# Half of the strided tensors loaded as whole 72 rows, the other half as 64 rows and a shared rest

## Chip, cores, metric

Trainium2, one core. The metric is the device time of one execution in microseconds (us).

## The reference, cut to what matters

```python
def reference(q, k, v, moe_w_r, moe_w_i, moe_w_ch):        # shortened by the author
    # q, k, v: [8 batches, 8 heads, 576, 64] float32; w_r, w_i: [64 modes, 512, 512]; w_ch: [512, 512]
    # heads 0..3: local mask (the last 32 positions); heads 4..7: strided mask (same position mod 32)
    attn = softmax(where(mask, q @ k^T / 8, -1e9)) @ v
    x = attn as [8, 576, 512]
    X = rfft(x, axis=1);  Y = zeros_like(X)
    Y[:, m] = X[:, m] @ (w_r[m] + 1j * w_i[m])             # 64 modes, each with its own weights
    u = x + irfft(Y)
    return u + relu(u @ w_ch)
```

The 64 modes' weights are most of what is loaded; the strided heads' inputs are loaded first.

Of the kernel before, what the change touches and what calls it, by code (L numbers as in the profile page):

```python
# [77 lines left out]
def kernel(  # L78
# [71 lines left out]
    ring = pat.tile([128, 12, 2048], F16, name="ring")  # L150
# [43 lines left out]



    SRC = {2: v, 0: q, 1: k}
    SLOT = {2: 0, 0: 1, 1: 2}

    def str_in(b, vi):  # L200
        return ring[0:72, 3 * (b % 4) + SLOT[vi], :]

    def loc_in(b, vi):
        t = ring[:, ds(2 * (b % 6), 2), :].rearrange("p n x -> p (n x)")
        return t[:, ds(1152 * vi, 1152)]

    def load_str(b):
        for vi in (2, 0, 1):
            nc.gpsimd.dma_start(
                str_in(b, vi)[0:64],  # L210
                SRC[vi][b, 4:8].rearrange("h (c r) d -> (h c) (r d)", r=32)[0:64],
            )
            if b % 2 == 0:
                n = 3 * (b % 4) + SLOT[vi]
                nc.gpsimd.dma_start(
                    ring[64:72, n : n + 4 : 3, :],
                    SRC[vi][b : b + 2, 4:8].rearrange(
                        "b h (c r) d -> (h c) b (r d)", r=32
                    )[64:72],
                )  # L220

    def load_loc(*bs):
        for b in bs:
            if b >= B:
                return
            for vi in (2, 0, 1):
                nc.gpsimd.dma_start(
                    loc_in(b, vi),
                    SRC[vi][b, 0:4].rearrange("h (cb i) d -> (h cb) (i d)", i=18),
                )  # L230
# [465 lines left out]

    psum_pools(tp=3, sc=3, av=2)
    load_str(0)
    const_load(nc.scalar, "cI", "cM6", "cM5", "cFs")
    load_str(1)  # L700
    const_load(nc.sync, "cMl", "cFl", "cA")
    load_str(2)
    w_fetch(2)

# [63 lines left out]
    for b in range(B):  # L768
# [12 lines left out]
        n = 0  # L781
        nm = NMODES[b]
        for mi in range(nm):
# [3 lines left out]
            n = upto  # L787
# [43 lines left out]
    n = 0  # L831
# [3 lines left out]
    for m in range(NM - 3):  # L835
# [7 lines left out]
        n = upto  # L843
# [99 lines left out]
    for i in range(len(units)):  # L943
        v_rows(i)
        b, t = units[i]
# [42 lines left out]
```

## The kernel before, where the change touches it

For a strided head, 576 positions are 18 rows of 32 positions. Four heads of one batch make 4 x 18 = 72 rows; one row is 32 x 64 numbers, read as float32 (8 KB) and written to SBUF as float16 (4 KB), one row to a partition. Each row is one packet in the trace (17,984 of 4,096 bytes on GpSimd's queue in the kernel before, as many as it has strided rows and weight rows). The kernel before loads the first 64 rows of each tensor alone, and the last 8 rows of two successive batches together ("the rest").

```python
    SRC = {2: v, 0: q, 1: k}
    SLOT = {2: 0, 0: 1, 1: 2}

    def str_in(b, vi):
        return ring[0:72, 3 * (b % 4) + SLOT[vi], :]
    # ... cut: loc_in
    def load_str(b):
        for vi in (2, 0, 1):
            nc.gpsimd.dma_start(
                str_in(b, vi)[0:64],
                SRC[vi][b, 4:8].rearrange("h (c r) d -> (h c) (r d)", r=32)[0:64],
            )
            if b % 2 == 0:
                n = 3 * (b % 4) + SLOT[vi]
                nc.gpsimd.dma_start(
                    ring[64:72, n : n + 4 : 3, :],
                    SRC[vi][b : b + 2, 4:8].rearrange(
                        "b h (c r) d -> (h c) b (r d)", r=32
                    )[64:72],
                )
```

The weights come on the same queue of GpSimd, each also as 64 rows of 4 KB:

```python
    def w_fetch(n=1):
        for _ in range(n):
            # ... cut: which buffer
            for ri, src in enumerate([moe_w_r, moe_w_i] if m else [moe_w_r]):
                nc.gpsimd.dma_start(
                    wt[ds(64 * ri, 64)],
                    src[m, ds(256 * half, 256), :].rearrange("(p c) e -> p c e", c=4),
                )
# ... cut
    load_str(0)
    load_str(1)
    load_str(2)          # constants between these are cut
    w_fetch(2)
# ... cut
    for b in range(B):   # the strided stage
        if b < 5:
            load_str(b + 3)
        load_loc(*[(), (), (), (), (0,), (1, 2), (3,), (4, 5)][b])
        w_fetch([3, 3, 2, 2, 2, 1, 1, 1][b])
        # ... cut: the attention of batch b
```

The softmax here doesn't subtract the row's maximum and nothing guards it: scores larger than these inputs give would overflow.

## Time and profile before

| kernel before | |
|---|---|
| time, first 3 runs | 439.35 us (439.08 to 439.46) |
| span of the profiled run | 437.8 us |
| moved by DMA, counted as written | 92.35 MB, mean 211 GB/s |
| GpSimd's DMA queue | 26,800 packets, 94.1% of 16 engines' time |
| 21st weight load complete | 63.24 us |
| last weight load complete | 396.36 us |

A load counts as complete when the last of its 16 completions has come. These are rows of the table of stretches of the kernel before; the last three columns are the granted TensorE clock, the mean busy share of the DMA engines (a row is recorded as 322 to 324 ns long and the next one starts 304 ns after it, so it can pass 1) and the GB/s moved.

```profile
11.00:22.00 11.00, 10.48 (x146) 9.07 (x145) 8.96 (x20) 7.04 (x14) 5.88 (x12) 1.00 1.06 210
22.00:33.00 11.00, 8.70 (x156) 7.11 (x157) 9.41 (x26) 9.07 (x20) 4.73 (x9) 1.00 1.06 212
33.00:44.00 11.00, 8.44 (x126) 7.25 (x126) 8.29 (x24) 7.07 (x16) 6.00 (x12) 0.84 1.06 210
```

A share of 1.06 with 210 to 212 GB/s is what full engines with undisturbed rows look like here.

### The profile page before, as it was taken

How to read it: one execution, taken by the hardware profiler on the slowest of the kernel's cores; microseconds unless marked ns; L12 is line 12 of the kernel's file. 1: busy time of each engine (PE TensorE's matmuls, PEld its weight loads, DVE VectorE, ACT ScalarE, POOL GpSimd, SP SyncE). 2: the span in 40 equal slices, each digit the busy share in tenths (PEclk: the TensorE clock that was granted, in tenths of full speed). 3: DMA queues.
4: the chain of work that ended last, by engine and by line, in shares of the span. 5: the costliest groups of instructions: out<-in, count | busy, mean ns of one | idle time of the engine just before them, and what ended most of it. 6: DMA issues, size and time to landing. Idle time of an engine off the chain costs nothing.

```text
span 437.8 us, 12314 instructions
## 1 busy us (share of the span) xinstructions
PE 338.0 (77%) x5284; PEld 240.9 (55%) x5284; DVE 215.6 (49%) x463; ACT 188.6 (43%) x353; POOL 186.8 (43%) x339
## 2 busy tenths in 40 slices
PE   1977787689895888989765475778586958997994
PEld 1866676567784666766644344445454635654441
DVE  2887788844543333353311134354335434753895
ACT  1686688625543445444432211134022402443882
POOL 6545453333344344444343444343444444310883
PEclk9998999967986657686875559696777868988998
DMA  8999999999999999999999999999999999990687
GB/s 186 211 211 212 211 213 209 211 210 211 213 211 212 213 208 211 213 212 211 211 212 211 213 212 210 213 213 210 201 211 212 211 212 213 211 192 15 264 324 277
DMA packets 31094, 92.35 MB, mean 211 GB/s; under 512 B 6144, under 2 KB 7040, under 8 KB 31040
## 3 DMA queue, kind: packets, MB, share of 16 engines
q0 software_dynamic: 26800, 81.29, 94.1%
q1 hardware_dynamic: 3440, 9.50, 5.8%
q10 hardware_dynamic: 800, 0.77, 0.6%
q8 instruction: 42, 0.69, 0.6%
q14 instruction: 12, 0.10, 0.1%
HBM read 163.37 MB, written 9.44 MB: 395 GB/s over the span
## 4 chain that ended last, share of the span: by engine, by line
DMA 74%; PE 15%; DVE 4%; issue 4%; POOL 1%; ACT 0%; DVEq 0%; POOLq 0%
DMA wt<-in_moe_w_i_dram 54%; DMA wt<-in_moe_w_r_dram 12%; DMA ring<-in_v_dram 4%; DMA ring<-in_q_dram 4%; PE sc L634 3%; PE v L884 2%; PE v L669 2%; PE u L684 2%; PE y L536 1%; DVE yy L663 1%; PE u L903 1%; PE tp L313 1%; POOL wt L183 1%; PE tp L642 1%; DVE xT L586 1%
## 5 line engine op out<-in xcount | busy, mean ns | idle before, releaser
L536 PE MATMUL y<-X,wt 128*128 128x16 f16 (+1 forms) x2048 | 82.2, 192 | 59.0 <-DMA wt<-in_moe_w_i_dram 57.1
L183 POOL DMA_DIRECT2D wt<-in_moe_w_r_dram x128 | 65.8, 514 | 118.8 <-DMA wt<-in_moe_w_r_dram 35.6
L536 PEld LDWEIGHTS <-wt 128*128 128x128 f16 (+1 forms) x2048 | 72.0, 103 | 72.7 <-issue 51.7
L183 POOL DMA_DIRECT2D wt<-in_moe_w_i_dram x126 | 64.8, 514 | 67.5 <-DMA wt<-in_moe_w_i_dram 50.0
L643 ACT ACTIVATE v<-sc 128x512 f16<-128x512 f32 x32 | 18.9, 597 | 88.4 <-PE sc L634 88.4
L634 PE MATMUL sc<-w_cp,xT 128*128 128x512 f16 (+1 forms) x160 | 52.5, 459 | 0.5 <-DVE xT L606 0.4
L460 ACT ACTIVATE PL<-sc 128x480 f16<-128x480 f32 (+1 forms) x48 | 27.5, 579 | 48.1 <-PE sc L446 47.8
L644 DVE COPY xo<-tp 128x512 f16<-128x512 f16 x32 | 22.1, 692 | 42.4 <-PE tp L642 42.4
L239 DVE TENSOR_TENSOR xb<-av,rec 90x256 f16<-90x256 f32 (+2 forms) x80 | 36.0, 450 | 2.7
L238 DVE RECIPROCAL rec<-av 90x4 f32<-90x4 f32 (+2 forms) x80 | 14.7, 184 | 40.1 <-PE av L475 29.3
L391 DVE COPY qT<-tp 128x576 f16<-128x576 f16 x16 | 12.0, 758 | 39.9 <-PE tp L384 37.0
L249 ACT ACTIVATE v<-tp 128x640 f16<-128x640 f16 (+1 forms) x24 | 19.4, 807 | 21.5 <-PE tp L418 18.1
L349 ACT ACTIVATE PL<-sc 90x360 f16<-90x360 f32 (+1 forms) x48 | 22.8, 490 | 9.8 <-PE sc L342 9.1
L897 POOL TENSOR_TENSOR rl<-rl,xo 128x512 f32<-128x512 f32 x16 | 18.4, 1159 | 20.2 <-ACT rl L895 19.4
L384 PE MATMUL tp<-cI_s,ring 64*64 64x64 f16 x864 | 26.1, 211 | 1.0 <-DVE qT L391 0.6
L914 DVE TENSOR_TENSOR osb<-u,rl 128x512 f32<-128x512 f32 x36 | 23.9, 689 | 3.1 <-ACT zz L662 1.9
L430 PE MATMUL sc<-cMl_s,cI_s 128*128 128x480 f16 (+1 forms) x48 | 23.1, 481 | 1.6 <-ACT X L249 1.6
L384 PEld LDWEIGHTS <-ring 64*64 64x64 f16 x864 | 20.7, 123 | 6.2 <-issue 3.4
L446 PE MATMUL sc<-qT,kz 128*128 128x160 f16 (+1 forms) x160 | 23.4, 275 | 0.8 <-issue 0.8
L634 PEld LDWEIGHTS <-xT 128*128 128x128 f16 (+1 forms) x160 | 14.8, 110 | 14.9 <-issue 7.2
L446 PEld LDWEIGHTS <-kz 128*128 128x128 f16 x160 | 16.7, 118 | 11.3 <-issue 8.8
L274 PE MATMUL tp<-cI_s,ring 72*128 72x72 f16 x256 | 15.1, 207 | 10.1 <-DMA ring<-in_v_dram 7.7
(98 smaller groups left out, 647.1 us busy)
## 6 DMA issues: line engine op xcount, KB each, us to landing
wt<-in_moe_w_r_dram POOLq DMA_DIRECT2D x128, 256.0 KB, 9.4
wt<-in_moe_w_i_dram POOLq DMA_DIRECT2D x126, 256.0 KB, 9.6
out_dram<-osb SPq DMA_DIRECT2D x14, 512.0 KB, 2.7
ring<-in_v_dram POOLq DMA_DIRECT2D x8, 288.0 KB, 10.3
ring<-in_q_dram POOLq DMA_DIRECT2D x8, 288.0 KB, 10.7
ring<-in_k_dram POOLq DMA_DIRECT2D x8, 288.0 KB, 10.3
ring<-in_v_dram POOLq DMA_DIRECT2D x8, 256.0 KB, 8.0
ring<-in_q_dram POOLq DMA_DIRECT2D x8, 256.0 KB, 8.3
```

The source lines that it names most:

```text
L183: nc.gpsimd.dma_start(wt[ds(64 * ri, 64)], src[m, ds(256 * half, 256), :].rearrange("(p c) e -> p c e", c=4),)
L239: nc.vector.tensor_tensor(out=dst, in0=val.rearrange("p h (q c) -> p h c q", c=4), in1=rec[0:n, 0:pieces] .to_broadcast((n, pieces, 64)) . ...
L249: nc.scalar.activation(out=out, in_=in_, func=ACTF.Copy)
L349: nc.scalar.activation(out=PS[0:n, ds(POFF[t], 4 * n)], in_=scp[0:n, 0 : 4 * n], func=ACTF.Exp, scale=SCALE,)
L384: nc.tensor.transpose(tp[ds(64 * hp, 64), ds(64 * i, 64)], qn[ds(64 * hp, 64), ds(64 * (9 * g + i), 64)], idn[ds(64 * hp, 64), ds(64 * hp, ...
L430: nc.tensor.matmul(scp[:, 0 : n * times].rearrange("p (h x) -> p h x", h=times), idn, mask_rows("cMl", n, times), start=True, stop=False,)
L446: nc.tensor.matmul(scp[:, ds(col, n)], kzs[par][:, hp, ds(s0, 128)], qTs[par][:, ds(s0, n)], start=False, stop=(i == len(todo) - 1),)
L460: nc.scalar.activation(out=dst, in_=src, func=ACTF.Exp, scale=SCALE)
L536: nc.tensor.matmul(yv[:, mi, e, :], wt[pr, XC[c], ds(128 * e, 128)], Xh[half][pr, c, :, :, m], start=(c == 0), stop=(c == 3),)
L634: nc.tensor.matmul(vp[pr, :], xT[:, ch, cols], w_chs["cp"][:, ch, :], start=(ch == 0), stop=(ch == 3),)
L644: nc.vector.tensor_copy(out=xo[pr].rearrange("p (h q c) -> p h q c", h=2, c=4), in_=tp[pr, 0:512].rearrange("p (h c q) -> p h q c", h=2, c=4),
L914: nc.vector.tensor_tensor(out=osb[:, t % 2, :], in0=up, in1=rls[b, t][:, t % 2, :], op=AluOp.add)
```

## The change

The intent is fewer DMA issues and fewer small transfers: half of the (batch pair, tensor) combinations load all 72 rows in one transfer, and only the other half keeps 64 rows and the shared rest.

```diff
     def load_str(b):
         for vi in (2, 0, 1):
+            n = 64 if (b // 2 + SLOT[vi]) % 2 == 0 else 72
             nc.gpsimd.dma_start(
-                str_in(b, vi)[0:64],
-                SRC[vi][b, 4:8].rearrange("h (c r) d -> (h c) (r d)", r=32)[0:64],
-            )
-            if b % 2 == 0:
-                n = 3 * (b % 4) + SLOT[vi]
+                str_in(b, vi)[0:n],
+                SRC[vi][b, 4:8].rearrange("h (c r) d -> (h c) (r d)", r=32)[0:n],
+            )
+            if n == 64 and b % 2 == 0:
+                i = 3 * (b % 4) + SLOT[vi]
                 nc.gpsimd.dma_start(
-                    ring[64:72, n : n + 4 : 3, :],
+                    ring[64:72, i : i + 4 : 3, :],
                     SRC[vi][b : b + 2, 4:8].rearrange(
                         "b h (c r) d -> (h c) b (r d)", r=32
                     )[64:72],
```

## The prediction

> **What bounds the kernel now.** I read the sliced part of the page first, for the engines and the DMA.
>
> ```profile
> PE   1977787689895888989765475778586958997994
> ...
> DMA  8999999999999999999999999999999999990687
> GB/s 186 211 211 212 211 213 209 211 210 211 213 211 212 213 208 211 213 212 211 211 212 211 213 212 210 213 213 210 201 211 212 211 212 213 211 192 15 264 324 277
> ...
> q0 software_dynamic: 26800, 81.29, 94.1%
> ```
>
> No compute engine is full for long, but the DMA engines are full from the second slice to the 35th (about 11 to 383 us), at 208 to 213 GB/s with one dip to 201. The software queue, which GpSimd feeds, carries 94% of it. The strided loads that change sit in the first 61 us of this stream; the weights follow on the same queue. Next the chain of work that ended last, from its late part:
>
> ```profile
> 326.86 0.28 issue
> 327.14 9.64 DMA wt<-in_moe_w_i_dram
> ...
> 356.60 0.28 issue
> 356.88 9.64 DMA wt<-in_moe_w_i_dram
> 366.65 0.65 PE y L536 x16
> 367.30 0.86 PE sc L634 x4
> ```
>
> Columns are start, length and what (us). Until 366.5 us the chain is one weight load after another; each is issued when the one eight places before it has landed (the Pool's DMAs use eight semaphores in turn), so one link of 9.64 us spans eight loads of 1.24 us that stream without a hole. From 366.65 us it is TensorE and VectorE work. The timeline of TensorE shows the change-over:
>
> ```profile
> 359.25 0.64 PE L536 MATMUL y<-X,wt 128*128 128x16 f16 x16 [1.28 <-DMA wt<-in_moe_w_i_dram]
> ...
> 366.65 0.65 PE L536 MATMUL y<-X,wt 128*128 128x16 f16 x16 [0.80 <-DMA wt<-in_moe_w_i_dram]
> ...
> 372.46 0.65 PE L536 MATMUL y<-X,wt 128*128 128x16 f16 x16
> ...
> 397.22 0.64 PE L536 MATMUL y<-X,wt 128*128 128x16 f16 x16
> ```
>
> The bracket is idle time and what ended it. Mode 51 (at 366.65) is the last that waits for its weights; its load landed at 366.52. What follows is a fixed tail of 437.8 - 366.6 = 71.2 us. So the kernel ends a fixed time after one landing, and whatever delays the DMA stream by x before then delays the end by x.
>
> **A closer reading of the landings.** Every load posts 16 completions, one from each DMA engine, and the trace's completion records show when. In the steady stage, first and last completion of one load lie 4.1 to 4.6 us apart: the 16 engines run at their own pace, and the slowest sets each landing. The packet records tell why. A 4 KB row follows the one before it on its engine after 304 ns, and a completion takes 21 ns: 4 x 304 + 21 = 1237 ns for a load of 64 rows over 16 engines, which is the 1.24 us step between landings. Following packets in chains, every engine gets 4 rows of every 64-row load. Of the 8-row rest (two batches, 16 rows) eight engines get 2 rows each and the other eight none, and the two halves take turns from rest to rest. Twelve rests make six turns each, so before is even: by the sizes, 17,984 rows over 16 engines are 1,124 each. What spreads the engines is 42 instruction fetches of 16 KB (about 0.95 us each), whose durations repeat with period eight: they fall on eight engines. Near 55 us the first and the last completion both belong to the half that is served second, and the fetch gaps that I could follow are on that half too. These eight late engines end within about 1.2 us of each other, at 395 to 396 us, the other eight at 392. The slowest never runs dry: where GpSimd was held up for 3.4 us near 152 us, the early engines lost their lead but the last landings kept their 1.24 us step.
>
> [...]
>
> **The change part by part.** Bytes are the same. The DMA issues:
>
> ```profile
> ring<-in_v_dram POOLq DMA_DIRECT2D x8, 256.0 KB, 8.0
> ring<-in_q_dram POOLq DMA_DIRECT2D x8, 256.0 KB, 8.3
> ring<-in_k_dram POOLq DMA_DIRECT2D x8, 256.0 KB, 8.3
> ...
> ring<-in_v_dram POOLq DMA_DIRECT2D x4, 64.0 KB, 7.7
> ring<-in_q_dram POOLq DMA_DIRECT2D x4, 64.0 KB, 7.3
> ring<-in_k_dram POOLq DMA_DIRECT2D x4, 64.0 KB, 6.9
> ```
>
> These are 24 loads of 64 rows and 12 rests. After: 12 loads of 64, 12 of 72, 6 rests.
> 1. Removed: six issues. On GpSimd that is 6 x 0.57 us = 3.4 us, but GpSimd waits for landings anyway, so nothing of it is on the path. On each DMA engine a rest costs up to two small packets, 2 x 21 ns: 6 x 42 = 0.25 us gained, on the path.
> 2. Moved: which engine carries the rows. [...]
> 3. If instead fourteen engines take 5 rows: 12 x 4 + 12 x 5 + 3 x 2 = 114 rows, 6 more than 108: 6 x 0.304 = 1.82, less 0.25: **+1.6 us**.
> 4. Earlier inputs: two batches' slots no longer have to be free before a rest is issued, for half of the rests, and half the tensors land in one piece. TensorE waits once for strided data for long (7.7 us at the start), but this stage ends far ahead of its weights; the first wait for weights comes later, so nothing on the path.
>
> **The rivals.** *The rows are spread evenly after all*[...]: then only part 1 remains, 439.1 us. For it: the change looks meant as a saving of issues; against it: 72 isn't a multiple of 16, and somebody chose 64 plus a rest. *Twelve engines*: 442.6 us[...]. *Sixteen engines with 5 rows*: 441.0[...]. *GpSimd is the limit at the start*, so that fewer issues start the stream earlier: in the timeline the first eight issues follow each other in 0.5 to 0.7 us each, and each 64-row load holds the engines for 1.24 us; the queue is never short, and I give it 0.3 us at most. *A longer lag empties the queue*: with 3.6 us more, the spread of 4 to 5.8 us would near the 9.9 us that eight loads hold; the early engines then stop more often, the late ones don't, so no further cost.
>
> **Range and chances.** Weights 0.35 for twelve engines (+3.3), 0.45 for sixteen with 5 rows (+1.6), 0.2 for an even spread (-0.2) give 0.35 x 3.3 + 0.45 x 1.6 - 0.2 x 0.2 = +1.8; I stay near the most likely case and put 441.0 us. The range from 438.9 to 443.0 holds all three with the scatter between runs, which was 0.4 us. A change of 2% is 8.8 us, over twice the largest of these: faster by over 2% has 0.01, slower by over 2% has 0.02, within has 0.97.
>
> **What would show it right or wrong.** The slices of DMA should stay at 208 to 213 GB/s, the chain should still run over weight loads until near 367 us plus the loss, and mode 51's neighbours should still be the last to wait. The last weight landing, now 396.4 us, should move by as much as the end. In the completion records the spread between first and last should be wider after the strided stage (after 61 us): by up to 3.6 us with twelve engines, by 2 with sixteen, with one engine that races ahead. In the packet records rows in a load of 72 should come as runs of 6 on twelve engines, or of 5. Wrong would be: an unchanged spread and the time at 439.1 (even spread); a time above 443.5 (the late engine runs dry, or the compute in the strided stage came onto the path); or a gain of over 1 us, which would mean that the row was taken off the engines that are late.

The kernel before has no load of 72 rows, so its trace doesn't say how they spread: the three cases and their weights are estimates. The forecast's sum: 0.35 x 3.3 (twelve engines) + 0.45 x 1.6 (part 3) - 0.2 x 0.2 (part 1 alone) = +1.8 us. It was put at part 3's +1.6, which is 441.0 us.

Two of its readings have more figures in the trace of the kernel before. Turns: two steps alternate. At its rests from the second on, the load's first completion came 0.33, 0.17, 0.50, 0.17, 0.50, 0.18, 0.62, 0.18, 0.59, 0.21 and 0.57 us after that of the transfer before. Instruction fetches: most durations follow 893, 948, 945, 935, 974, 974, 961, 893 ns and again from the start; that they fall on eight engines is read from this period. 42 x 0.95 / 8 = 5.0 us on each of these, beside a spread of 4.1 to 4.6 us, so that they are what spreads the engines is an estimate.

## More of the kernel before

The experiments ran on three chips (e1 to e4 on one, e5 to e11 on another, e12 and e13 on a third), each beside the kernel before on the same chip; each loss is taken against that chip's own runs of it. Of the kernel before there is one profile, so counts from profiles are compared across chips.

All strided inputs but the three of the last batch (in by 70.1 us) are in before the 21st weight load, so its time is the state of the stream near the end of the stage that the change touches.

## The result and the profile after

| | before | after |
|---|---|---|
| median of 6 runs | 439.40 us (438.39 to 439.86) | 443.42 us (442.33 to 445.02) |
| span of the profiled run | 437.8 us | 441.5 us |
| 21st weight load complete | 63.24 us | 68.00 us (+4.8) |
| last weight load complete | 396.36 us | 401.57 us (+5.2) |

The ratio is 1.010, 95% interval 1.0075 to 1.0125: slower by 1%, inside the 2% that counts as the same. A ratio here and below is the mean time of one kernel's fast runs over the mean of the other's of the same rounds, so it is not quite the ratio of the medians quoted. The +4.0 us lie above the predicted +1.6 and 0.4 us above the range.

First the page of the changed kernel, the sliced lines and the queue:

```profile
DMA  8999999999999999999999999999999999991687
GB/s 179 181 197 200 210 196 202 211 211 212 211 211 211 214 210 205 209 215 211 213 209 212 212 213 211 212 213 212 210 190 211 212 212 211 212 212 37 264 316 279
...
q0 software_dynamic: 26704, 81.29, 94.6%
```

The busy digits of the early slices are unchanged: 9 from the second on. But the GB/s of the first seven slices read 179 to 202 with one 210, where before they were 209 to 213 from the second on. Engines as busy as before move less. From the eighth slice on both kernels look alike. The queue has 96 packets fewer and yet takes 94.6% of a longer span.

The stretches of the changed kernel say it more sharply (columns as above):

```profile
11.00:22.00 11.00, 9.34 (x112) 8.39 (x110) 7.11 (x15) 4.78 (x9) 4.78 (x9) 1.00 1.12 180
22.00:33.00 11.00, 9.41 (x172) 7.71 (x170) 9.21 (x25) 9.04 (x19) 3.80 (x8) 1.00 1.09 196
33.00:44.00 11.00, 8.58 (x155) 6.77 (x151) 9.41 (x26) 8.31 (x19) 4.92 (x10) 1.00 1.07 202
```

In the first row the DMA share went up from 1.06 to 1.12 while the rate fell from 210 to 180. Busy time per byte is share over rate: (1.12 / 180) / (1.06 / 210) = 1.23, so a byte cost 23% more engine time. In the next two rows it is 11% and 5%. If engines had only been short of work, or some had more rows than others, the share would have fallen with the rate. So packets took longer.

The packet records give the same thing row by row. A 4 KB row of GpSimd's queue is recorded as lasting 322 to 324 ns in both kernels (its neighbours start 304 ns apart). Of those in the first 80 us, 32 of 3,456 lasted over 344 ns before, and 689 of 3,357 after, 368 of them over 400 ns. I call these slow rows; of the 689, 574 lasted from 345 to 500 ns.

The completion records also show how 72 rows are spread. These are, for four loads of the changed kernel in their order, the 16 completions in us after the load's first:

```
before, 8th   0.0 0.4 0.8 0.9 0.9 1.1 1.1 1.1 1.1 1.2 1.2 1.3 1.5 1.5 1.8 1.8
after,  7th   0.0 0.4 2.6 2.6 2.7 2.8 2.9 3.0 3.0 3.2 3.2 3.3 3.3 3.7 3.7 3.9
after,  9th   0.0 1.4 4.6 4.7 4.7 4.8 4.9 5.0 5.1 5.2 5.3 5.4 5.4 5.7 5.8 5.9
after, 12th   0.0 1.6 5.8 5.9 5.9 6.1 6.1 6.2 6.2 6.2 6.3 6.4 6.6 6.6 7.2 7.3
```

Two engines race ahead, one more than the other, and fourteen stay together; twelve engines with 6 rows would have left four ahead. At the 12th, after four loads of 72, the two lead the third by 5.8 and 4.2 us, or 1.45 and 1.05 us a load: at 304 ns a row that is about 5 and 3 to 4 rows. So I read the 72 rows as 5 on fourteen engines, 2 on one and none on one.

The issues, from the view of the DMA:

```profile
ring<-in_q_dram POOLq DMA_DIRECT2D x12, 288.0 KB, 10.5
ring<-in_v_dram POOLq DMA_DIRECT2D x12, 288.0 KB, 10.4
ring<-in_k_dram POOLq DMA_DIRECT2D x12, 288.0 KB, 10.7
...
ring<-in_v_dram POOLq DMA_DIRECT2D x2, 64.0 KB, 7.4
```

The x12 are the 8 local inputs of each tensor and four whole 72-row loads, which happen to have the same size; of the rests two are left per tensor. All as intended.

The late chain keeps its form, one link per eight weight loads, and the change-over to TensorE comes 5.3 us later (366.65 before). From the chain and from TensorE's timeline of the changed kernel:

```profile
352.32 9.62 DMA wt<-in_moe_w_i_dram
362.22 9.64 DMA wt<-in_moe_w_i_dram
```

```profile
371.99 0.65 PE L538 MATMUL y<-X,wt 128*128 128x16 f16 x16 [0.43 <-DMA wt<-in_moe_w_i_dram]
374.87 0.66 PE L538 MATMUL y<-X,wt 128*128 128x16 f16 x16
```

The chain's shares differ more than its end does. The line of the page before and the line after:

```profile
DMA 74%; PE 15%; DVE 4%; issue 4%; POOL 1%; ACT 0%; DVEq 0%; POOLq 0%
```

```profile
DMA 63%; PE 23%; DVE 6%; issue 4%; ACT 1%; POOL 1%; DVEq 0%; POOLq 0%; ACTq 0%
```

The extra compute in the chain stands between 73 and 122 us: there a load was issued when TensorE freed a buffer, not when an earlier load landed. It is no loss by itself: slices 8 to 12 are at 211 to 212 GB/s, so the engines still had work. Of the +5.2 us at the last weight load, 4.8 were there at 68 us.

### The profile page after: what moved, and what is told of

It reads as the page before. It is cut to its first block, busy times and chain, and to the rows that moved or that the text cites. A ratio compares the mean times of both kernels' runs of the same rounds, so it can differ in the third digit from the quotient of the medians.

```text
span 441.5 us, 12303 instructions
## 1 busy us (share of the span) xinstructions
PE 345.9 (78%) x5284; PEld 247.5 (56%) x5284; DVE 215.8 (49%) x463; ACT 189.0 (43%) x353; POOL 183.6 (42%) x333
## 3 DMA queue, kind: packets, MB, share of 16 engines
q0 software_dynamic: 26704, 81.29, 94.6%
## 4 chain that ended last, share of the span: by engine, by line
DMA 63%; PE 23%; DVE 6%; issue 4%; ACT 1%; POOL 1%; DVEq 0%; POOLq 0%; ACTq 0%
DMA wt<-in_moe_w_i_dram 50%; DMA ring<-in_v_dram 6%; DMA wt<-in_moe_w_r_dram 5%; PE y L538 3%; PE sc L636 2%; DMA ring<-in_q_dram 2%; PE v L886 2%; PE v L671 2%; PE u L686 2%; PE tp L276 1%; PE tp L386 1%; PE tp L315 1%; PE sc L344 1%; DVE xb L241 1%; PE sc L336 1%
## 5 line engine op out<-in xcount | busy, mean ns | idle before, releaser
L505 PEld LDWEIGHTS <-xb 108*128 108x128 f16 (+2 forms) x176 | 17.4, 115 | 9.8 <-issue 5.2
```

## The experiments

The theory that I formed from the profile after is **place**: how long a row takes depends on the partitions that it is written to and on those that the rows beside it are written to. The 64-row loads of the kernel before write 0 to 63 or, for w_i, 64 to 127; a 72-row load writes 0 to 71, with 5 rows on most engines where the others have 4. If loads with different maps of rows to partitions are in flight together, rows may get in each other's way. The records name neither the engine nor the partition of a packet, so this is a reading and not an observation. Why writes should clash, I had taken from an assumption on the way from an engine to SBUF, with an estimate of the time of a slow row; no trace shows it. What I expected of place: +7 to +9 us in e1, +3.5 to +5 in e2, +1 to +3 in e3 and "as before" in e12.

The rivals: **count** (six rows more on fourteen engines, 1.6 us by the prediction's step 3, and the rest scatter); **order** (the last 8 rows come at other times, waits move); **source** (reads from HBM collide); **any shift** (any two different maps clash, however far the one is shifted).

A summary of the runs first. "Slow rows" are those over 344 ns in the first 80 us; "landing" is the last weight load's completion in the profiled run, less 396.36; time is median less the median of the kernel before in the same rounds.

| run | slow rows | landing, us | time, us | ratio, 95% |
|---|---|---|---|---|
| before | 32 | 0 | 0 | 1 |
| the change | 689 | +5.2 | +4.0 | 1.0075 to 1.0125 |
| the change again (e8) | 720 | +5.3 | +4.8 | 1.0093 to 1.013 |
| e1: all 24 as 72 rows | 228 | +5.4 | +4.8 | 1.0091 to 1.013 |
| e2: 80 rows for 72 | 403 | +3.4 | +2.9 | 1.0046 to 1.008 |
| e3: half moved by 8 partitions | 703 | +3.6 | +3.6 | 1.0067 to 1.013 |
| e4: 64 + own rest for 72 | 60 | +1.5 | +0.9 | 1.0007 to 1.005 |
| e5: 56 + 16 for 72 | 339 | +4.3 | +4.4 | 1.0084 to 1.0121 |
| e6: half read 8 rows later | 176 | +1.1 | -0.3 | 0.9967 to 1.0021 |
| e9: turns | 205 | +2.2 | +2.4 | 1.0033 to 1.0088 |
| e10: turns, the other way | 133 | +2.2 | +1.5 | 1.0016 to 1.0055 |
| e11: all moved by 8 | 479 | +3.7 | +2.8 | 1.0041 to 1.0085 |
| e12: half moved by 32 | 52 | +0.2 | +0.4 | 0.9987 to 1.002 |
| e13: four more loads | 275 | +6.8 | +7.2 | 1.0147 to 1.0189 |

(e7 was built wrongly and is told below: +7.6 us.) All give the reference's result except e6 and e12. Their outputs are wrong, which doesn't matter for the times.

### e1_all72: every strided tensor as one load of 72 rows

```diff
-                str_in(b, vi)[0:64],
-                SRC[vi][b, 4:8].rearrange("h (c r) d -> (h c) (r d)", r=32)[0:64],
+                str_in(b, vi)[0:72],
+                SRC[vi][b, 4:8].rearrange("h (c r) d -> (h c) (r d)", r=32)[0:72],
-            if b % 2 == 0: ... the rest is gone
```

> All 24 strided loads whole with 72 rows, no rests: the change at twice its dose. Imbalance alone (5 rows on fourteen engines, 24 x 5 = 120 rows against 108, 12 x 0.304 us = 3.65 us, less 0.5 us for the removed small packets): +3.1 us over before, about 442.5. [...] the loss of the change, 4.0 us, doubles: +7 to +9 us, about 447, and the slices of DMA throughput stay under 200 GB/s while strided loads come in.

443.83 against 439.02 us: +4.8, no more than the half-way change costs. Two rows of its stretches:

```profile
33.00:44.00 11.00, 9.47 (x135) 7.82 (x135) 8.51 (x24) 7.11 (x15) 3.64 (x7) 0.84 1.05 204
44.00:55.00 11.00, 7.55 (x121) 6.40 (x119) 7.37 (x20) 6.62 (x15) 4.28 (x9) 0.83 1.03 200
```

Here the share falls with the rate, which I read as engines with few rows that idle. With 24 x 5 = 120 rows on each of fourteen engines, by the spread read in the change, against 108, count alone makes 12 x 0.304 = 3.6, less 0.5 for the removed rests, +3.1. The remaining 1.7 come with 228 slow rows, a third of the change's. So twice the dose of 72-row loads gives more by count and less by slow rows: it may be that loads of one map disturb each other less than two kinds in turn; this run alone doesn't show it. Neither of the two written expectations, count alone (+3.1) and place (+7 to +9), came true.

### e2_80: 80 rows where the change loads 72

```diff
+            m = 80 if n == 72 and b < B - 1 else n
-                str_in(b, vi)[0:n], SRC...[0:n]        (as in the change)
+                ring[0:m, 3 * (b % 4) + SLOT[vi], :],
+                SRC[vi].rearrange("b h (c r) d -> (b h c) (r d)", r=32)[r0 : r0 + m],
```

80 rows should be 5 on each of 16 engines, so that no engine is left out, and the busiest has as many rows as in the change (12 x 4 + 12 x 5 + 3 x 2 = 114). Eight rows are loaded for nothing in ten of the twelve loads.

> The whole loads made longer, 80 rows in place of 72 (ten of twelve; the last two stay 72): 5 rows on every one of the 16 engines, so the busiest engine has as many rows as in the change and no engine runs ahead. The 8 extra rows are never read. Imbalance alone: as the change by its row count, +1.6 us, about 441.0. Theory that the two engines which run ahead cause the loss (their share is idle, the queue of eight runs dry): +1.6 us at most. [...] the loss stays at +3.5 to +5 us, 443 to 444.5, with rows over 400 ns in hundreds.

441.87 against 439.02 us: +2.9, with 403 slow rows. By this count the busiest engine carries what it does in the change, but the loss is 1.1 to 1.9 us smaller, and slow rows are fewer. It lies between the two expectations, +1.6 by count and +3.5 to +5 by place, so both missed. In the change two engines lead the third by 6.0 us at the 16th load; here the first two are 0.5 us ahead of the third. That engines out of step make more rows slow would fit, but is argued. If the counts are right, the busiest engine's count doesn't set the loss alone.

### e3_shift8: no 72-row load at all, half the tensors placed 8 partitions further

Here the counts are those of before. The same half of the tensors loads its 64 rows into partitions 8 to 71 and its rest into 0 to 7.

```diff
+            a = 0 if (b // 2 + SLOT[vi]) % 2 == 0 else 8
-                str_in(b, vi)[0:64],                    # source likewise
+                str_in(b, vi)[a : a + 64],
-                    ring[64:72, n : n + 4 : 3, :],      # source likewise
+                    ring[z : z + 8, i : i + 4 : 3, :],  # z = 64 - 8 * a
```

> Row counts, engines, issues and shared rests exactly as before; only for the half of the pairs that the change touches, the 64 rows are those of partitions 8 to 71 and the rest is partitions 0 to 7. Each engine still gets 4 rows[...]. Imbalance alone or fewer issues: no change, 439.4 within 0.5 us. [...] +1 to +3 us, with some hundred rows over 400 ns in the strided stage, against some 15 before.

442.58 against 439.02 us: +3.6, with 703 slow rows. Sizes, issues and order are those of before (and with them, I take it, the rows per engine), and yet nearly the whole loss is there. Two rows of its stretches:

```profile
11.00:22.00 11.00, 10.46 (x140) 9.26 (x141) 8.18 (x19) 6.24 (x12) 5.24 (x11) 1.00 1.16 178
22.00:33.00 11.00, 9.22 (x166) 7.53 (x166) 9.64 (x26) 9.12 (x21) 4.63 (x9) 1.00 1.06 207
```

A share of 1.16 with 178 GB/s is the change's sign, stronger. Order can't make it, nor count if the rows per engine are the same. The loss is above the +1 to +3 that I had expected of place.

### e4_ownrest: the 72-row loads as 64 rows and an own rest of 8

```diff
-                str_in(b, vi)[0:n], ...                 (as in the change)
+            for a, z in [(0, 64)] + ([(64, 72)] if n == 72 else []):
+                    str_in(b, vi)[a:z], ...
```

> The pairs that the change loads whole as 64 rows and an own rest of 8 rows for each batch (not shared by two): same bytes, same arrival order and same waits for free slots as the change, but no load of 72. If the loss came from the order of arrival or from the waits for slots, it stays: +2 to +4 us. If it comes from the form of the 72-row load[...], it goes: 439.0 to 440.0. A side effect is possible: should the rests of one batch always go to the same eight engines, these carry 6 rows more and the others 6 fewer than in an even spread, so the time moves by 1.8 us, down if they are the eight that are early, up if they are the late ones.

439.93 against 439.02 us: +0.9, 60 slow rows. The same tensors are complete at the same places of the order as in the change, so order and moved waits are not the cause. The 0.9 may have a cause of their own in the completion records: between the 20th, 22nd and 25th load, with one own rest in each gap, the ninth completion falls behind the first by 0.99, 1.27 and 1.59 us. So own rests seem to put their rows always on the same half of the engines, the one that is behind, while shared rests take turns. No run isolates this.

### e5_56_16: 72 rows as 56 and 16

```diff
+            for a, z in [(0, 64)] if n == 64 else [(0, 56), (56, 72)]:
+                    str_in(b, vi)[a:z], ...
```

> The twelve loads of 72 as 56 and 16 rows. By the spread seen for 72[...], 56 rows go to fourteen engines, 4 each[...], and 16 rows to sixteen, 1 each: again 5 rows on fourteen engines, 1 on the other two[...]. Imbalance alone: as the change by count, +1.6 us and up to +0.5 for twelve more issues, 441 to 441.5, with few rows over 400 ns. If two engines that run ahead were enough for the slow rows: +4 us, 443.4, with over 500 rows above 400 ns.

443.83 against 439.46 us: +4.4, with 339 slow rows. I had meant it as a measure of count without slow rows, and it is none: the 56- and 16-row loads together make slow rows themselves. Which engine writes which of the 56 rows I haven't settled. The 16-row piece goes to partitions 56 to 71. The run separates nothing.

### e6_src: as e3, but only the reads move (wrong result)

```diff
-                SRC[vi][b, 4:8].rearrange("h (c r) d -> (h c) (r d)", r=32)[0:64],
+                SRC[vi][b, 4:8].rearrange("h (c r) d -> (h c) (r d)", r=32)[a : a + 64],
-                    )[64:72],
+                    )[z : z + 8],
```

> Wrong on purpose (rows land in other partitions than they belong to). The same rows of memory are read by the same engines in the same order as in the run shifted by 8, but they are written to partitions 0 to 63 and 64 to 71 as in the kernel before. If the slow rows come from where they are written[...]: back to before, 439.0 within 0.7 us, about 15 rows over 400 ns. If they come from where they are read in memory: +3.6 us as in the run shifted by 8, with about 700 rows over 400 ns.

439.21 against 439.46 us: no loss (interval -0.3% to +0.2%); 176 slow rows. Two rows of its stretches, to set beside e3's:

```profile
11.00:22.00 11.00, 10.55 (x149) 9.28 (x146) 8.83 (x20) 6.81 (x13) 5.97 (x12) 1.00 1.08 200
22.00:33.00 11.00, 8.88 (x160) 7.15 (x157) 9.41 (x26) 9.05 (x21) 4.23 (x9) 1.00 1.06 212
```

The same rows are read in the same loads as in e3, but written where before writes them. So it is the place of the writes that costs. The rival "source" falls as the main cause. Something is left over: 101 rows lasted over 400 ns where about 15 were expected, the first row above is at 200 GB/s, and in the profile the last weight load came 1.1 us later. Why is open.

### e7_early, e9_early and e10_late: which half is late

These were to test another of the prediction's steps: that a row more on one half of the engines costs, and on the other is hidden. A tiny transfer (8 partitions, 16 numbers each) before some rests was meant to make the rests' turn fall on the other half.

```diff
+    def take_turn(b, vi):          # t is a tile of its own in e9 and e10; one tile for all in e7
+        nc.gpsimd.dma_start(t[64:72, :, 0:8], SRC[vi][b : b + 2, 4:8]...[64:72, :, 0:8])
+                if (b, vi) in TURNS:
+                    take_turn(b, vi)
```

> The kernel before with six tiny transfers (8 rows of 2 x 16 bytes) between the rests, which take a turn of the eight engines each: nine rests instead of six fall on the eight engines that are early, three on the eight that are late. If the end is set by the rows on the late engines: 6 rows x 0.304 us = 1.8 us less on them, about 0.5 us more for the tiny packets: -1.3 us, 437.7 against 439.0. If the late engines are the other half: +1.8 us or more. If the balance between engines does not matter: 439.0 to 439.5.

e7 gave 447.04 against 439.46 us, and is worthless: all tiny transfers wrote one tile, so each waited for the one before, and GpSimd stood still (5.7 us once, 4.7 us once). Mended:

> The kernel of the run e7 mended: there all tiny transfers wrote one tile, so each waited for the landing of the one before and GpSimd stood still (5.7 us once, 4.7 us once). Now each has its own tile. Nine rests fall on the eight early engines, three on the late. If the end is set by the rows on the late engines: -1.8 us + 0.5 us = -1.3 us against before, 438. If the balance between engines does not matter: +0 to +0.5.

> The same with the first tiny transfer ahead of the first rest, so that nine rests fall on the eight late engines and three on the early ones. Same transfers, same sizes as in the run e9. If the end is set by the rows on the late engines: 12 rows x 0.304 us = 3.6 us above e9, 441.5 to 442; that is +1.8 + 0.5 = +2.3 us over before. If the balance does not matter: as e9.

e9 gave 441.67 and e10 440.72, against 439.27 us. Expected were -1.3 and +2.3 over before; measured are +2.4 and +1.5, and the two don't differ clearly: their intervals overlap, and in the profiles their last weight loads land together (398.56 and 398.51 us). Nor do the completions, which name no engine, show that the turns fell as planned. In both runs most of the rests that I followed push the late completions: e9's 18th transfer moves the first by 0.24 us and the last by 0.61, e10's 16th by 0.19 and 0.83. The half that gets nine rests may be behind for that reason alone. The tiny transfers also take places among the eight in flight: the 21st weight load came at 65.5 and 65.2 us against 63.2. I count it as inconclusive; the step "late half" is neither shown nor refuted in size.

### e8_again: the change once more

```diff
+            n = 64 if (b // 2 + SLOT[vi]) % 2 == 0 else 72       # and the rest of the change's diff
```

> The changed kernel itself once more, on the chip of these runs, for a ratio of the same rounds: +4.0 us, 443.0 to 443.5, ratio 1.009 to 1.010.

444.24 against 439.46 us, +4.8, 720 slow rows. With the +4.0 of the first measurement the loss is 4 to 5 us.

### e11_allshift: all tensors placed 8 partitions further

```diff
-                str_in(b, vi)[0:64],                    # source likewise
+                str_in(b, vi)[8:72],
-                    ring[64:72, n : n + 4 : 3, :],      # source likewise
+                    ring[0:8, n : n + 4 : 3, :],
```

> All 24 strided loads at partitions 8 to 71 and all rests at 0 to 7, where the run e3 shifted half of them. If rows get slow where loads of two different maps[...] are in flight together: the strided loads now agree among themselves and clash only with the weights, so fewer slow rows than the 712 of e3 (200 to 400) and a smaller loss, +1 to +2.5 us. If a shifted load or a rest at partitions 0 to 7 is slow in itself: twice the dose, some 1,400 slow rows and +6 to +7 us.

442.09 against 439.27 us: +2.8, 479 slow rows. Twice the displaced loads of e3 give no more than e3: fewer slow rows (703 there) but longer ones (476 ns in the mean against 429), and a loss of 2.8 against 3.6, on different chips and with overlapping intervals. So a displaced load is not slow in itself, which would have meant 1,400 slow rows and +6 to +7. This fits that it takes a load of another map beside it. But the figures are also above the 200 to 400 rows and +1 to +2.5 that I had expected of place; that what is left is the meeting with the weights, which keep the map of before, is argued and not shown.

### e12_shift32: half moved by 32 partitions (wrong result)

```diff
+            a = 0 if (b // 2 + SLOT[vi]) % 2 == 0 else 32
-                str_in(b, vi)[0:64],
+                ring[a : a + 64, n, :],
-                    ring[64:72, n : n + 4 : 3, :],
+                    ring[a + 64 : a + 72, n : n + 4 : 3, :],
+    for n in (1, 4, 6, 8, 9, 11):
+        nc.vector.memset(ring[0:32, n, :], 0.0)
```

If any shift hurts, this one should hurt like e3. Of place I had expected no loss here.

> Wrong on purpose: the half of the pairs that the run e3 displaced by 8 partitions is displaced by 32 (rows 0 to 63 to partitions 32 to 95, the rest to 96 to 103), and TensorE goes on reading partitions 0 to 71. [...] as before, 439.3 within 0.7 us, at most 200 slow rows in the first 75 us. If any displacement slows rows: +3.6 us and some 700 slow rows as in e3.

438.58 against 438.15 us, ratio 1.0004 (0.9987 to 1.002): no loss, 52 slow rows. A row of its stretches, to set beside e3's with 178:

```profile
11.00:22.00 11.00, 8.86 (x122) 7.80 (x121) 7.50 (x17) 5.55 (x10) 6.54 (x13) 1.00 1.07 212
```

A shift by 8 costs 3.6 us, one by 32 nothing. The rival "any shift" falls, and the result is the one expected of place. What a shift by 8 has that one by 32 lacks, no run shows: this one also moves half of each displaced load to 64 to 95, beyond the 0 to 63 of the other 64-row strided loads, so more room and the distance itself aren't told apart.

### e13_count: four more loads of 56 rows that nobody reads

```diff
+        if b % 2:
+            nc.gpsimd.dma_start(
+                xb[...][0:56].rearrange("p t x -> p (t x)")[:, 0:2048],   # into a free tile
+                k[b, 4:8].rearrange("h (c r) d -> (h c) (r d)", r=32)[0:56],
+            )
```

It was to price rows alone: 4 loads x 4 rows x 0.304 = 4.9 us more on the busiest engines.

> The kernel before with four extra loads of 56 rows in the strided stage (never read): 4 rows each on fourteen engines[...], none on the other two; 16 rows more on the busiest engines. If the end is set by the count on the busiest engines: 16 x 0.304 + 4 x 0.021 = +4.9 us, 444.2, and few slow rows (under 200). If the mean over the 16 engines counts: +4.3 us. If the count on single engines is absorbed by the lead of the others: under +2 us.

445.36 against 438.15 us: +7.2. But 275 slow rows came in bursts at the added loads (14 to 19, 29 to 31 and near 55 us), and the count term isn't isolated. After the first of these loads two engines are 1.1 us ahead of the other fourteen (4 x 0.304 = 1.2), so fourteen do get the rows. If these write where they always write, as I had assumed, the place theory has no reason for the slow rows (under 200 were expected). Either they write elsewhere or the theory lacks something; this stays open.

No experiment gave a version that beats the kernel before.

## Why the prediction was wrong

**Bound and end: right.** The DMA stream is the bound, and the change-over from waiting weights to the tail stayed at mode 51, 5.3 us later.

**Part 1 (removed issues are worth 0.25 us): not seen separately.** The queue's 96 packets fewer for six rests are 16 a rest, or one for each of 16 engines, where up to two were put. GpSimd has six instructions fewer and 3.2 us less busy time (183.6 against 186.8), which nothing waited for. That much was right.

**Parts 2 and 3 (how 72 rows are spread): the third case came.** Fourteen engines stay together, by the reading above with 5 rows each; twelve engines with 6 is ruled out by the completions. The rival that was given +3.3 is nearer to the measured time but not its cause.

**The step that failed is the sum of part 3**: "12 x 4 + 12 x 5 + 3 x 2 = 114 rows, 6 more than 108: 6 x 0.304 = 1.82, less 0.25: +1.6 us". It prices every row at 304 ns, as the undisturbed stream showed, and starts from "Bytes are the same". What it lacks is a term for rows that become slower because of where they are written; by the author's reading, because loads with different maps of rows to partitions are in flight together. In the changed kernel that is 689 rows over 344 ns against 32. The term alone, with no load of another size, is +3.6 us in e3. In the change it is what 4.0 to 4.8 leave over 1.6: some 2.4 to 3.2 us by difference. A rough estimate from the packet records makes it more: the slow rows' time above 324 ns, summed over the first 80 us and divided by 16 engines, is 5.2 us in the change, 4.6 in e3 and in e11, and 0.2 before. In e3 and e11, whose counts are those of before, the extra 4.4 and 4.3 us made the 21st weight load 3.4 and 3.8 us later; at that rate the change's extra 5.0 are 3.8 to 4.4 of its 4.8. So the split isn't measured: e5 and e13, meant to isolate the count, both made slow rows of their own, and e3's slow rows are about as many as the change's, but the records don't tell on which engines either fall. What is shown is that displaced writes alone make slow rows and lose time (e3, +3.6), that displaced reads make no loss (e6, -0.3), that a displacement by 32 partitions makes none (e12, +0.4), and that the order of arrival explains at most 0.9 (e4). That different maps in flight together are the reason is a reading of these four and not shown by itself; why a shift by 8 clashes and one by 32 doesn't is not shown at all, and e13's slow rows don't fit as it stands.

**"The slices of DMA should stay at 208 to 213 GB/s": wrong**, and the plainest sign: 179 to 202 in six of the first seven. The prediction's list of what would put the time above 443.5 held only a dry engine and compute on the path. A packet that takes longer at a full engine wasn't on it.

**"The last weight landing should move by as much as the end": not quite.** It moved 5.2 us, the end 3.7 in the profiled runs. From that landing to the end took 41.4 us in the profile of before and 39.9 after. In the other profiles it was 39.4 to 41.0, so the "fixed tail" scatters by 2 us and the profile of before is its long end. The loss by timed medians, 4.0 and 4.8 us, lies between the two.

**Spread after the strided stage: right in kind.** At the 21st weight load first and last completion lie 4.7 us apart, before 2.1; two engines lead the other fourteen, as step 3's case has it, and the spread is 2.6 us wider, where it expected 2. At the last weight load it was 3.1 us (before 4.3): leaders lose their lead when GpSimd holds up the queue, as for 3.4 us at 165 us in the chain, where the spread fell from 5.5 to 3.5 us.

**Range: too narrow at the top.** All three cases behind it were counts at one row price, and their largest was 442.6.

## What to carry to other kernels

In this kernel, with its DMA stream full, the place that rows are written to had a cost of its own: 178 against 210 GB/s with the same rows in as many loads of the same sizes (e3). It is worth trying to keep the rows per engine, and the partitions that they go to, the same in all transfers that are in flight together, and to price a new shape by the rate of its stage, not by the row time of the old shape. A busy digit of 9 beside a falling GB/s line meant slow packets here (the change), and a share that fell with the rate fits idle engines (e1); read the two together. An odd split such as 64 and a shared rest of 8 can be there to keep that map: with 64 and an own rest of 8, e4 had 60 slow rows against the change's 689.
